# Loading x for a convolution by FFT: one chunk of the inverse per piece, and the last nine rows in one transfer per batch

## The chip, the cores and the metric

The kernel runs on one core of a Trainium2 chip. The metric is the time of one execution on that core in microseconds (us); lower is better. The core has a matrix engine (PE, with its weight loads shown apart as PEld), a vector engine (DVE), a scalar engine (ACT), a general engine (POOL) and a queue engine (SP), which run side by side and wait for each other through semaphores, and 16 DMA engines that move data for all of them.

## The reference

Two parts, one after the other. The first convolves each of 128 channels of `x` along the sequence with `h`, causally, by FFTs of twice the length. The second takes that result as its `x`, turns it by an angle, mixes it over the sequence with two matrices of 5696 x 5696 and ends with a small layer over the channels.

```python
batch, seq, d_model = (8, 5696, 128)
...
L = 2 * S
Xf = np.fft.rfft(x, n=L, axis=1)
Hf = np.fft.rfft(h, n=L, axis=0)
y = np.fft.irfft(Xf * Hf[None, :, :], n=L, axis=1)[:, :S, :]
...
theta = x @ w_theta
zr, zi = x * np.cos(theta), x * np.sin(theta)
y = np.einsum('ts,bsd->btd', w_tok_r, zr) + np.einsum('ts,bsd->btd', w_tok_i, zi)
u = x + y
return (u + np.maximum(u @ w_ch, 0.0)).astype(np.float32)
```

## The kernel before

The convolution takes the first 350 to 400 us of the span, and the change touches only this part. The sequence of 5696 is seen as 89 rows of 64, and the transform of length 11392 as 178 times 64. The work is cut into eight groups: a pair of batches and one half (64) of the channels. Each group goes through four stages.

- Stage a (`stage_a`, line 250): for each of the 64 channels one matmul takes the group's slice of x, 89 partitions by 128 columns (two batches of 64), against a table of 89 x 180. All four pieces of both batches must have landed before the first of these matmuls can run. ACT moves the results to the tile `a` (line 259).
- Stage b (`stage_b`, with `f2`, line 270): the second transform, in 12 chunks of up to 8 frequencies, each with 32 small matmuls. ACT moves a chunk to `xs` (line 426), and DVE multiplies it with the spectrum of h, `hs` (lines 428 and 433), into `uv`. `hs` comes from the scratch `hf_hbm` in HBM, 256 KB per chunk, by transfers of the SP queue (line 419). There are four buffers for `hs` (`LEAD`), so four chunks are loaded ahead and every further one starts when DVE has used an earlier one.
- Stage c (`stage_c`, lines 448 and 449): the first half of the inverse, in 16 chunks of 8 columns. Each chunk is moved to the tile `g` by DVE (line 455) or ACT (line 453).
- Stage d (`stage_d`, line 484): the second half of the inverse, in 7 chunks, moved to `yt` (lines 488 and 490) and stored to `yt_hbm` by eight transfers of the SP queue (line 497).

The loop over the groups has two halves. In the first half, stage c of group g is woven with stage a of group g+1, with the first four `hs` loads of group g+1 and with the loading of x for group g+2. In the second half, stage b of group g+1 is woven with stage d of group g. Below, "a stage c" and "a stage b" mean these halves, numbered by the loop. The helper `woven` sorts the steps of its lists by place: a list with (0.1, 1.02) is spread evenly from 10% to 102% of the half.

x is loaded by `load_x`. A group's tile `x16` has 89 partitions, two batches, 64 columns and 64 channels, in half precision, and there are two such tiles. The transfers convert from single precision, and POOL issues them. They come in eight pieces: four for each batch, 16 of the 64 columns each. A piece is two transfers, of the first 80 rows and of the last 9, and every row and column of it is a run of 64 numbers of its own. Before a piece of a group from the third on, POOL copies one number of `g` into the piece (line 151). This copy has no use but to wait: the transfer of the 80 rows, which writes over that number, can't start before the chunk of stage c that made it. The number is that of column `16 * i`, which is in chunk 2i, so piece i waits for chunk 2i. The 9 rows lie in other partitions, so they don't wait for it.

The queue of POOL runs in order. For the first two groups and in the first half of the loop's first turn, the order on DVE, ACT and POOL is that of the text. After that a planner puts each engine's instructions in order. It lets the 9-row transfers of a group run ahead of that group's copies, so that most of them stand at the end of the loop's first half one turn earlier. There they wait until stage a has read the tile that they overwrite (line 250). Every transfer that POOL issues also waits for the one eight before it, since eight semaphores are used in turn.

After the eight groups, the mixing over the sequence fills the rest of the span; its weights come in by POOL's transfers as well (line 676).

Of the kernel before, what the change touches and what calls it, by code (L numbers as in the profile page):

```python
# [22 lines left out]
def kernel(  # L23
# [10 lines left out]
    nc = tc.nc  # L34
    B, S, D = x.shape
# [40 lines left out]
    N2 = 64  # L76
    N1 = NF // N2
    NB = S // N2
    K1 = N1 // 2 + 1
    CK = 8  # L80
    HD = D // 2
# [48 lines left out]
    for p0, p1 in ((0, 80), (80, NB)):  # L130
        nc.gpsimd.dma_start(u_t[p0:p1, :N2 * D],
                            bass.AP(tensor=h.tensor, offset=h.offset + p0 * N2 * D,
                                    ap=[[N2 * D, p1 - p0], [1, N2 * D]]))
# [3 lines left out]
    def load_x(g, after=None):  # L137

        bp, dh = divmod(g, 2)
        if g >= B:  # L140
            return []
        if g not in x16s:
            x16s[g] = fx.tile([P, 2, N2, XP], F16, tag="x16", name="x16")
        x16 = x16s[g]

        def piece(i):
            e, n0 = i // 4, i % 4 * 16
            src = x[2 * bp + e]
            if after is not None:
                g_ = after["g"]  # L150
                nc.gpsimd.tensor_copy(x16[0:1, e, n0, 0:1], g_[0:1, 0, 16 * i:16 * i + 1])  # L151
            for p0, p1 in ((0, 80), (80, NB)):
                nc.gpsimd.dma_start(  # L153
                    x16[p0:p1, e, n0:n0 + 16, :HD],
                    bass.AP(tensor=src.tensor, offset=src.offset + (p0 * N2 + n0) * D + dh * HD,
                            ap=[[N2 * D, p1 - p0], [D, 16], [1, HD]]))
        return [lambda i=i: piece(i) for i in range(8)]

    ordered = ExitStack()
# [120 lines left out]
    def woven(*lists):  # L280

        lists = [l if isinstance(l, tuple) else (l, 0.0, 1.0) for l in lists]
        steps = [(w0 + (i + 0.5) / len(l) * (w1 - w0), n, f)
                 for n, (l, w0, w1) in enumerate(lists) for i, f in enumerate(l)]
        for _, _, f in sorted(steps, key=lambda s: s[:2]):
            f()
# [97 lines left out]
    def e_table(n):  # L384
        n0 = 11 * n
        t, k, r = ((e_y[0], e_f[1], e_y[0]), (e_y[1], e_y[0], e_y[1]), (e_f[2], e_y[1], e_y[0]))[n]
        nc.vector.tensor_scalar(k, t, MAGIC, None, op0=add)
        nc.vector.scalar_tensor_tensor(r, k, MAGIC, t, op0=ALU.subtract, op1=ALU.subtract)
        absolute(k, r)

        def curves():
            t3, k3 = (z.rearrange("p (n m) -> p n m", m=NB) for z in (r, k))
            sine(e_t[:K1, n0:n0 + 11, 1, :], t3, -1)
            cosine(e_t[:K1, n0:n0 + 11, 0, :], k3)
        return curves

    def swap_rows():
        for c0 in range(0, NCK, NCK // 2):
            for ri in range(2):
                dst, src = (hf_hbm[c0:c0 + NCK // 2, :, r0:r0 + 64, r, :].rearrange("c h p n -> (c h) p n")  # L400
                            for r0, r in ((64, ri), (0, 1 - ri)))
                nc.sync.dma_start(dst, src)
# [36 lines left out]
    def stage_c(st, last):  # L439

        def chunk(q):
            if q == 0:
                st["g"] = fg.tile([P, 2 * N2, P], F16, tag="g", name="g_")
            ps = psum()
            for i in range(8):
                o = ps[:, i // 4, (i % 4) * P:(i % 4 + 1) * P]
                at = (q + i) * K1
                nc.tensor.matmul(o, u_t[:, at:at + P], r_u, start=True, stop=False)  # L448
                nc.tensor.matmul(o[:, 2 * NP:], v_t[:, at:at + P], r_v, start=False, stop=True)  # L449
            g_out = st["g"][:K1, :, q:q + 8]  # L450
            g_in = ps[:K1].rearrange("p a (q c) -> p c (a q)", q=4)
            if (last and q % 16 == 0) or (not last and q % 32 == 16):
                nc.scalar.activation(g_out, g_in, AF.Copy)
            else:
                nc.vector.tensor_copy(g_out, g_in)
        return [lambda q=q: chunk(q) for q in range(0, 2 * HD, 8)]
# [48 lines left out]
    def front(g, by_dve=(), a_=None, spare=None):  # L505
        if g >= len(groups):
            return [], [], []
        bp, dh = groups[g]
        x16 = x16s[g].rearrange("p b n d -> p (b n) d")
        steps, a_st = stage_a(lambda q: x16[:NB, :, q], by_dve, a_, spare)  # L510
        return (steps, *stage_b(a_st, dh, WARM if g else WARM // 2, g == 0))
# [142 lines left out]
    def open_ring():  # L654

        ring["all"] = keep.tile([P, K1 * 3 * N2], BF16, tag="keep", name="ring")
        pump()
# [27 lines left out]
    def open_phases():  # L685
        st = sides["phases"] = {}
        sb1 = pool("s2", 2, pha, reuse_waits="tile")
        st["sb1"] = sb1
        st["zz"] = pool("s2z", ZB, pha, reuse_waits="tile")
        sbc = pool("s2c", 1, pha, reuse_waits="tile")  # L690
        for w_, dst, mul in ((moe_w_theta, w_theta_sb, 1.0 / (2.0 * math.pi)), (moe_w_ch, w_ch_sb, 1.0)):
            t = sbc.tile([P, P], F32, tag="wt", name="wt")
            nc.gpsimd.dma_start(t, w_[:, :])
            nc.gpsimd.tensor_scalar(dst, t, mul, None, op0=mult)
        ones = sbc.tile([P, P], BF16)
        nc.vector.memset(ones, 1.0)
        pm = sbc.tile([P, 2], BF16)
        nc.vector.memset(pm[:, 0:1], MAGIC / P)
        nc.vector.memset(pm[:, 1:2], -MAGIC / P)
        plus, minus = (pm[:, q:q + 1].to_broadcast([P, 512]) for q in range(2))  # L700
        w_neg = sbc.tile([P, P], BF16)
        nc.gpsimd.tensor_scalar(w_neg, w_theta_sb, -1.0, None, op0=mult)
        st["turns"] = (ones, plus, minus, w_neg)

    def load_ya0():
        sides["phases"]["ya0"] = only = ExitStack()
        ya = sides["phases"][0] = pool("s2a", 1, only, reuse_waits="tile").tile([P, 4, H], BF16, name="ya0")
        for p_ in range(4):
            nc.gpsimd.dma_start(ya[:, :, p_ * QR:p_ * QR + QR], yt_hbm[:, 0:4, p_ * QR:p_ * QR + QR])
# [54 lines left out]
    def with_load(step, load):  # L764
        def both():
            step()
            if load:
                ring["upto"] += 1
                pump()
        return both  # L770

    for g, (bp, dh) in enumerate(groups):
        st = {}
        last = g + 1 == len(groups)
        a_, load_, b_ = fronts.pop(g + 1) if g + 1 in fronts else front(g + 1)
        if last:
            for _ in range(3):
                steps0.pop(0)()
        now = ([with_load(steps0.pop(0), n < 6) for n in range(9)] if last else [], 0.0, 0.88)
        c_ = stage_c(st, last)  # L780
        if g == 0:
            ec = []
            swap_rows()
            now = ([lambda: ec.append(e_table(1)), lambda: ec.pop()(), lambda: ec.append(e_table(2)), lambda: ec.pop()(),
                    e_minus],
                   -0.1, 0.6)
        woven((c_, 0.06 if a_ else 0.0, 1.0), (a_, 0.0, 0.88), now, load_, (load_x(g + 2, st), 0.1, 1.02))
        if g == 0:
            ordered.close()
        if g + 2 == len(groups):  # L790
            xin.close()
            open_phases()
            load_ya0()
        now = [steps0.pop(0) for _ in range(5)] if last else []
        woven(b_, (stage_d(st, bp, dh, load_ya1 if last else None), 0.08 if b_ else 0.0, 1.1 if b_ else 1.0), now)
        if g + 2 == len(groups):
            load_ya1(st["yt"], True)
            open_ring()
# [305 lines left out]
    nxt, second, st = None, None, {}  # L1104
    ordered = ExitStack()
    for i, (k, p, tt, j0, s0, nj) in enumerate(stretches):
# [13 lines left out]
        if (p, tt, j0 + s0) == (0, 1, 0):  # L1120
            with tc.issue_after(sides["late"].ins):
# [4 lines left out]
        woven = (tt is not None and end_of_pair and i + 1 < len(stretches)  # L1126
                 and stretches[i + 1][2] is not None)
        held = a if i else None
        a, nxt = nxt, None if i == 1 else prepare(i + 1, not woven)
# [208 lines left out]
```

## Time and profile before

| | |
|---|---|
| median of 3 runs | 2052.54 us (2051.28 to 2053.35) |
| the profiled execution | 2052.18 us |
| its span in the profile | 2050.4 us |
| PE busy | 1959.6 us, 96% of the span |
| DVE, POOL, ACT busy | 1538.9, 965.2, 639.9 us |
| mean granted clock of PE | 0.987 |
| x's transfers (line 153) | 128, 97.9 us of POOL |
| of 80 rows | 64, 160 KB each, median 5.0 us from issue to landing |
| of 9 rows | 64, 18 KB each, median 4.7 us |
| the copies that wait (line 151) | 48, six groups of 8 |

Times are in us from the start of the span, unless marked ns. A line of the timeline has the start, the length, the engine, the line, the operation with what it writes and reads, how many were merged, and in square brackets how long the engine stood idle before and what ended that. "issue" there means that nothing the profile shows was waited for. A view by stretches of time gives the busy time of each engine in each stretch, the mean clock that was granted to PE, and the busy share of the 16 DMA engines, which goes above 1 where packets overlap on an engine. In a view of the DMA queues, q0 is POOL's transfers, q1 is those of SP, and q8 is the fetching of instructions.

### The profile page before, as it was taken

How to read it: one execution, taken by the hardware profiler on the slowest of the kernel's cores; microseconds unless marked ns; L12 is line 12 of the kernel's file. 1: busy time of each engine (PE TensorE's matmuls, PEld its weight loads, DVE VectorE, ACT ScalarE, POOL GpSimd, SP SyncE). 2: the span in 40 equal slices, each digit the busy share in tenths (PEclk: the TensorE clock that was granted, in tenths of full speed). 3: DMA queues.
4: the chain of work that ended last, by engine and by line, in shares of the span. 5: the costliest groups of instructions: out<-in, count | busy, mean ns of one | idle time of the engine just before them, and what ended most of it. 6: DMA issues, size and time to landing. Idle time of an engine off the chain costs nothing.

```text
span 2050.4 us, 42565 instructions
## 1 busy us (share of the span) xinstructions
PE 1959.6 (96%) x16205; PEld 1086.2 (53%) x16381; DVE 1538.9 (75%) x2806; ACT 639.9 (31%) x936; POOL 965.2 (47%) x1769
## 2 busy tenths in 40 slices
PE   7799899799999999999999998999999999999998
PEld 5688888654444444444444443444444444444444
DVE  7787777657788888787867667867777686777767
ACT  6788777872232333333300000011111111111111
POOL 8323312384354545454566454453544535354450
PEclk9899999999999999999999999999999999999999
DMA  9999996999899998999999799797887969788793
GB/s 151 187 180 159 146 171 204 238 293 179 163 179 176 170 180 159 179 173 177 170 168 159 119 251 217 107 152 131 150 145 132 155 124 153 131 150 146 131 156 85
DMA packets 510158, 338.21 MB, mean 165 GB/s; under 512 B 184136, under 2 KB 461256, under 8 KB 509864
## 3 DMA queue, kind: packets, MB, share of 16 engines
q0 software_dynamic: 322368, 157.47, 61.0%
q1 hardware_dynamic: 181600, 166.48, 27.8%
q10 hardware_dynamic: 5984, 11.54, 1.6%
q8 instruction: 128, 2.10, 0.4%
q14 instruction: 78, 0.63, 0.1%
HBM read 379.54 MB, written 95.63 MB: 232 GB/s over the span
## 4 chain that ended last, share of the span: by engine, by line
PE 66%; DVE 3%; DMA 2%; issue 1%; POOL 0%; ACT 0%; DVEq 0%; ACTq 0%; SPq 0%
PE m L1275 62%; DMA b<-z_hbm 1%; DVE c L1282 1%; DVE b L831 1%; PE v L977 1%; PE utp L970 1%; PE m L1279 1%; DVE wt L890 1%; PE theta_ps L560 0%; PE tpz L918 0%; PE m L1162 0%; PE m L1196 0%; POOL ring L676 0%; DMA c<-cp_hbm 0%; DMA wl<-in_moe_w_tok_i_dram 0%
## 5 line engine op out<-in xcount | busy, mean ns | idle before, releaser
L676 POOL DMA_DIRECT2D ring<-in_moe_w_tok_i_dram x720 | 387.9, 546 | 657.7 <-DVE wt L890 576.9
L890 DVE STREAM_TRANSPOSE wt<-ring 128x384 f32<-128x384 f32 (+2 forms) x720 | 360.5, 527 | 127.7 <-PE m L1275 77.7
L676 POOL DMA_DIRECT2D ring<-in_moe_w_tok_r_dram x720 | 386.2, 547 | 142.4 <-DVE wt L890 82.4
L1275 PE MATMUL m<-b,wt 128*128 128x512 bf16 x1605 | 386.6, 380 | 3.7 <-DVE wt L890 1.7
L1275 PEld LDWEIGHTS <-wt 128*128 128x128 bf16 x1804 | 176.3, 98 | 219.5 <-DVE wt L890 7.4
L1282 DVE TENSOR_TENSOR c<-c,m 128x512 f32<-128x512 f32 x412 | 266.8, 674 | 0.4 <-PE m L1275 0.4
L972 ACT ACTIVATE ring<-utp 128x512 bf16<-128x512 bf16 x85 | 50.8, 597 | 582.1 <-PE utp L970 582.1
L428 DVE TENSOR_TENSOR uv_t<-xs,hs 128x2048 f16<-128x2048 f16 x88 | 104.4, 1224 | 29.9 <-ACT xs L426 18.2
L448 PE MATMUL ps<-r_u,uv_t 128*128 128x128 f16 x1024 | 116.5, 219 | 4.7 <-ACT cos L588 1.3
L1196 PE MATMUL m<-b,wt 128*128 128x512 bf16 x471 | 110.3, 379 | 7.6 <-DMA b<-z_hbm 4.2
L967 ACT ACTIVATE ub<-c 128x512 bf16<-128x512 f32 x88 | 55.1, 628 | 192.1 <-DVE c L1237 113.5
L449 PE MATMUL ps<-r_v,uv_t 128*128 128x100 f16 x1024 | 114.1, 207 | 0.5
L153 POOL DMA_DIRECT2D x<-in_x_dram x128 | 97.9, 771 | 22.2 <-POOL x L151 14.9
L426 ACT ACTIVATE xs<-ps 128x1024 f16<-128x1024 f32 x96 | 90.8, 972 | 42.4 <-PE ps L270 21.9
L449 PEld LDWEIGHTS <-uv_t 128*128 128x128 f16 x1024 | 99.9, 98 | 7.1 <-issue 5.7
L448 PEld LDWEIGHTS <-uv_t 128*128 128x128 f16 x1024 | 100.0, 98 | 1.1 <-DVE uv_t L433 0.4
L1196 PEld LDWEIGHTS <-wt 128*128 128x128 bf16 x528 | 50.4, 98 | 65.1 <-issue 8.4
L562 ACT ACTIVATE red<-theta_ps,magic 128x512 f32<-128x512 f32 (+1 forms) x46 | 31.6, 687 | 153.1 <-PE theta_ps L560 80.4
L270 PEld LDWEIGHTS <-w_t 64*128 64x128 f16 x3240 | 59.4, 100 | 32.1 <-issue 23.3
L920 ACT ACTIVATE ring<-tpz 128x512 bf16<-128x512 bf16 (+1 forms) x46 | 27.5, 597 | 132.6 <-PE tpz L918 116.3
L250 PE MATMUL ps<-f_t,x 89*128 89x180 f16 x512 | 62.8, 252 | 2.1 <-DVE a L257 1.1
L831 DVE TENSOR_TENSOR b<-b 128x1024 bf16<-128x1024 bf16 x100 | 61.4, 685 | 0.0
(2924 smaller groups left out, 3746.7 us busy)
## 6 DMA issues: line engine op xcount, KB each, us to landing
ring<-in_moe_w_tok_r_dram POOLq DMA_DIRECT2D x352, 96.0 KB, 4.6
ring<-in_moe_w_tok_i_dram POOLq DMA_DIRECT2D x352, 96.0 KB, 4.9
ring<-in_moe_w_tok_r_dram POOLq DMA_DIRECT2D x352, 80.0 KB, 4.5
ring<-in_moe_w_tok_i_dram POOLq DMA_DIRECT2D x352, 80.0 KB, 4.0
cp_hbm<-c SPq DMA_DIRECT2D x88, 256.0 KB, 2.6
c<-cp_hbm SPq DMA_DIRECT2D x88, 256.0 KB, 4.5
out_dram<-c SPq DMA_DIRECT2D x88, 256.0 KB, 4.5
hs<-hf_hbm SPq DMA_DIRECT2D x84, 256.0 KB, 3.4
```

Source lines behind the costliest of these rows:

```text
L153: nc.gpsimd.dma_start(x16[p0:p1, e, n0:n0 + 16, :HD], bass.AP(tensor=src.tensor, offset=src.offset + (p0 * N2 + n0) * D + dh * HD, ap=[[N2 ...
L250: nc.tensor.matmul(ps[:, i // 2, (i % 2) * 2 * K1:(i % 2 + 1) * 2 * K1], lhs(q + i), f1_t[:NB], start=True, stop=True)
L426: nc.scalar.activation(xs[:, :, :, :ck], ps, AF.Copy)
L428: nc.vector.tensor_tensor(uv[:, :, :, c0:c0 + ck], xs.rearrange("p e d k -> p e (d k)").unsqueeze(1).to_broadcast([P, 2, 2, HD * CK]), hv. ...
L448: nc.tensor.matmul(o, u_t[:, at:at + P], r_u, start=True, stop=False)
L449: nc.tensor.matmul(o[:, 2 * NP:], v_t[:, at:at + P], r_v, start=False, stop=True)
L676: nc.gpsimd.dma_start(wb[32 * i:32 * i + 32, :ng, :nj * 64], bass.AP(tensor=a.tensor, offset=a.offset + row0 * S + p * H + i * QR + j0 * 6 ...
L831: return [lambda f=f, x=x: f(*x) for f, x in ((nc.vector.tensor_sub, (bt[M3], b12, b22)), (nc.vector.tensor_sub, (bt[M4], b21, b11)), (nc. ...
L890: nc.vector.transpose(wt.rearrange("p j t r -> p (j t r)").bitcast(F32).rearrange("p (j g t) -> p g j t", j=TJ, g=4)[:, :ng, :nj], wb[:, : ...
L1196: nc.tensor.matmul(ms[n // 2 * 2 + h], a[n][:, j, :, r], bts_of[p][jj][n % 2 * 2 + h][:, r, :], start=(n % 2 == 0 and jj == 0 and r == 0), ...
L1275: nc.tensor.matmul(ms[q], a[q][:, j, :, r], bts[jj][q][:, r, :], start=(jj == 0 and r == 0), stop=(jj == NJ - 1 and r == 1 and q not in left))
L1282: nc.vector.tensor_tensor(c, z, ms[q], op=op)
```

## The change

The number that a piece waits for is that of column `8 * i` in place of `16 * i`, so piece i waits for chunk i. The list of pieces is spread over 10% to 60% of the half in place of 10% to 102%. The first three pieces of a batch load 80 rows only, and with the fourth the last 9 rows of all 64 columns come in one transfer. A group has 10 transfers in place of 16, of the same bytes and the same runs.

```diff
             if after is not None:
                 g_ = after["g"]
-                nc.gpsimd.tensor_copy(x16[0:1, e, n0, 0:1], g_[0:1, 0, 16 * i:16 * i + 1])
-            for p0, p1 in ((0, 80), (80, NB)):
+                nc.gpsimd.tensor_copy(x16[0:1, e, n0, 0:1], g_[0:1, 0, 8 * i:8 * i + 1])
+            for p0, p1, a, w in ((0, 80, n0, 16), (80, NB, 0, N2))[:2 if i % 4 == 3 else 1]:
                 nc.gpsimd.dma_start(
-                    x16[p0:p1, e, n0:n0 + 16, :HD],
-                    bass.AP(tensor=src.tensor, offset=src.offset + (p0 * N2 + n0) * D + dh * HD,
-                            ap=[[N2 * D, p1 - p0], [D, 16], [1, HD]]))
+                    x16[p0:p1, e, a:a + w, :HD],
+                    bass.AP(tensor=src.tensor, offset=src.offset + (p0 * N2 + a) * D + dh * HD,
+                            ap=[[N2 * D, p1 - p0], [D, w], [1, HD]]))
         return [lambda i=i: piece(i) for i in range(8)]
...
-        woven((c_, 0.06 if a_ else 0.0, 1.0), (a_, 0.0, 0.88), now, load_, (load_x(g + 2, st), 0.1, 1.02))
+        woven((c_, 0.06 if a_ else 0.0, 1.0), (a_, 0.0, 0.88), now, load_, (load_x(g + 2, st), 0.1, 0.6))
```

In the two built programs the order of instructions on PE, DVE, ACT and SP is the same; only POOL's differs. In the turns from the second on, POOL has: the first four copies each followed by its 80-row transfer, then two copies, two transfers, two copies, two transfers, and at the end both 9-row transfers of the group that is loaded in the next turn, the first of which waits for stage a. In the first turn, where the order is by hand, the planner still puts the next group's 9-row transfers in: the first of them, which waits for stage a, stands behind the sixth copy and ahead of the sixth, seventh and eighth piece, as one of the smaller ones does before. The last two 9-row transfers of that kind fall away in the sixth turn in both programs, since there is no further group.

## The prediction

> **What bounds the kernel now.** First the view by stretches of time, cut where one loop half ends and the next begins (first and last matmul of line 449). PE is the engine to watch. The stages c from the second turn on last 17.46 us each, and PE is busy in all of it. The stages b that follow (rows below) differ:
>
> ```profile
> core 0: us, PE busy (x) PEld busy (x) DVE busy (x) ACT busy (x) POOL busy (x), PEclk, DMA share, GB/s
> 112.17:129.63 17.46, 17.46 (x310) 17.44 (x311) 12.96 (x11) 14.53 (x20) 8.09 (x16) 1.00 1.31 178
> 129.63:149.89 20.26, 17.95 (x571) 15.61 (x568) 16.80 (x16) 16.11 (x19) 5.21 (x9) 1.00 0.92 169
> ...
> 167.35:188.11 20.76, 17.99 (x571) 15.67 (x567) 16.81 (x16) 15.78 (x19) 4.96 (x9) 1.00 0.89 161
> ...
> 205.57:229.78 24.21, 20.23 (x571) 17.86 (x567) 16.97 (x16) 15.79 (x19) 4.95 (x9) 0.86 0.76 133
> ...
> 247.24:268.29 21.05, 17.70 (x571) 15.52 (x567) 16.87 (x16) 15.80 (x19) 4.95 (x9) 1.00 0.83 153
> ...
> 285.75:304.74 18.99, 17.78 (x570) 15.64 (x567) 16.78 (x16) 15.74 (x19) 1.66 (x3) 1.00 0.81 168
> ```
>
> The same 571 matmuls take 20.26, 20.76, 24.21, 21.05 and 18.99 us. The last, and shortest, is the one stage b into which POOL issues no row of nine (x3 in place of x9). Over it the four others hold 1.27 + 1.77 + 5.22 + 2.06 = 10.32 us.
>
> What the four wait for shows in the timeline of the weight loads, here in the longest:
>
> ```profile
> 210.11 0.89 PEld L484 LDWEIGHTS <-g__4597 90*128 90x128 f16 x21 [0.35 <-issue]
> 211.06 0.52 PEld L270 LDWEIGHTS <-w_t 64*128 64x128 f16 x32
> 211.64 1.25 PEld L484 LDWEIGHTS <-g__4597 90*128 90x128 f16 x30
> 212.96 0.72 PEld L270 LDWEIGHTS <-w_t 64*128 64x128 f16 x45
> 217.12 0.55 PEld L270 LDWEIGHTS <-w_t 64*128 64x128 f16 x19 [3.44 <-issue]
> ```
>
> PE stops in the middle of a run of equal loads, for "issue": it waits for no other engine. From 210.11 to the stop it took 21 + 32 + 30 + 45 = 128 loads, so with their matmuls 256 instructions. A 16 KB packet of q8 starts at 214.70 and takes 1.07 us, and PE goes on 1.35 us after its end. I counted all loads and semaphore steps of PE up to each stop: the stops at 140.1, 144.6, 175.0, 178.9, 213.7, 255.6, 328.0 and 335.6 stand at place 193 or 194 of 256, and each ends 1.35 to 1.71 us after a 16 KB packet of q8. So PE runs out of instructions. In stage b it uses 256 in 3.4 to 4 us; in stage c (311 loads in 17.46 us) in 7.2 us, and there it never stops.
>
> The view of the DMA queues for 206.3 to 213.8 says what the fetch stands behind:
>
> ```profile
> q0 software_dynamic: 4141, 0.43, 97.4%
> q1 hardware_dynamic: 333, 0.62, 33.6%
> q8 instruction: 1, 0.02, 0.8%
> ...
> x<-in_x_dram POOLq DMA_DIRECT2D x6, 18.0 KB, 5.7
> ```
>
> x's small runs fill the engines, and `hs` lands behind them. q0's last packets come 9.2, 8.9, 10.3 and 8.6 us after the end of stage c in those four turns, and 5.3 us in the sixth, where no fetch is late.
>
> **The change, part by part.** POOL's timeline of the second turn gives the prices:
>
> ```profile
> 118.97 0.18 POOL L151 COPY x<-g__2471 1x1 f16<-1x1 f16 x1 [1.00 <-DVE g__2471 L455]
> 119.49 0.89 POOL L153 DMA_DIRECT2D x<-in_x_dram  x1 [0.34 <-POOL x L151]
> ...
> 127.73 0.61 POOL L153 DMA_DIRECT2D x<-in_x_dram  x1 [0.70 <-PE ps L250]
> ...
> 130.41 4.43 POOL L153 DMA_DIRECT2D x<-in_x_dram  x7
> ```
>
> *The wait for chunk i.* A piece costs POOL 0.18 + 0.34 + 0.89 = 1.41 us, and chunks come every 17.46 / 16 = 1.09 us, so POOL sets the pace. The first copy stays at 114.47 and the eighth piece is issued by 114.47 + 8 x 1.41 = 125.8, where it is now issued at 131. Two pieces wait for a copy of the next one (1 us); the limit of eight transfers in flight is not reached before the tail.
>
> *Nine rows in one transfer.* POOL issues 10 per group in place of 16. One of 576 runs is not in the trace: between 0.61 us (144 runs) and 0.89 (1280) I take 0.72, by the line between. The two of the next group wait for stage a at 127.73 as one does now, and are out at 129.2; seven more transfers now take until 134.8. Behind them in POOL's queue stands only the next turn's copy, 15 us later. In all POOL saves 48 x 0.61 - 16 x 0.11 = 27.5 us, which lies beside PE's work and is worth nothing by itself.
>
> *When x is in.* Up to 122 SP's stores and `hs` loads share the engines: q0 has 2216 packets from 117 to 122. Of a group's 12544, 10328 are left, at 946 per us (2838 from 122 to 125) or 731 (2193 from 126 to 129): done at 132.9 to 136.1, so 3.3 to 6.5 us after stage c, about where the sixth turn has it. The `hs` loads of stage b start at 134, and the late fetches were 7.6 to 10.5 us after stage c. So I set the four stages b near 18.99. Least: only stops that begin while q0 still has packets go, 0.93 + 3.44 + 2.80 = 7.2. Most: all 10.3. I take -8.7, the middle.
>
> *The first turn.* There the 9-row transfer that waits for stage a blocks three pieces until 88.0, now and then. What follows is the same bytes, issued by 88.0 + 3 x (0.89 + 0.72) + 2 x 0.18 = 93.2 in place of 97.7. This stage b (22.26 us) waits mostly in the order between PE and ACT; its one stop at place 194 is 0.49. I take -0.4, between -3.3 (down to 18.99) and +1.0 (a stop like that at 140.1).
>
> *The start.* The first group's 16 transfers take POOL 13.09 us, and ten will take 13.09 - 6 x 0.61 = 9.4; the second group is issued from 23.3 on and not from 26.96. The engines are idle there (65 packets of q0 from 23.9 to 28.2). Four us at the 566 per us of 28.2 to 42 move 2300 packets forward, out of the 4737 that now share 42 to 54.7 with the stores and loads of h's spectrum. DVE starts there on
>
> ```profile
> 54.69 4.74 DVE L428 TENSOR_TENSOR uv_t<-xs,hs 128x2048 f16<-128x2048 f16 x4 [4.53 <-DMA hs<-hf_hbm]
> ```
>
> This wait and the next (1.44) can give up to 6.0 us. Against that, PE has two stops in fetching at 24.0 and 27.3 (1.50 and 2.13) while q0 is idle, and x now flows there: up to +3.6. I take -2.5.
>
> The rest of the span runs after this in the same order; I take 0. Sum: -8.7 - 0.4 - 2.5 = -11.6. The profiled execution took 2052.18 us (2050.4 and 1.8 around it), 0.36 under the median, so the forecast is 2040.6.
>
> [...]
>
> **The rivals.**
>
> 1. *x is not out in time.* With eight transfers in flight and `hs` among them, x drains until 8 us after stage c, as now. For: 946 per us was held for 3 us only, and 4491 packets from 130 to 138.9 are 505 per us. Against: there POOL issued seven transfers of 144 runs at 0.63 us each, 230 per us, so the issue set that pace. Half the first term and 1 us of the start are left: 2052.18 - 4.4 - 1.0 = 2046.8.
>
> 2. *The stops are not x's doing.* For: the stops at 144.6 and 178.9 come 5.8 and 2.6 us after q0's last packet, and that at 328 has no x near. Against: the sixth turn has none. The start alone remains: 2052.18 - 2.5 = 2049.7.
>
> 3. *Slower: the fetch is late in stage c too.* With pieces every 1.41 us q0 is never empty there. [...] For: the DMA share in stage c goes from at most 1.54 toward what two pieces at once make (2.16 from 122 to 125). Against: at 2.16 no stop is seen in any stage c, and there the next packet of q8 comes in time.
>
> That the change does not do what it says is excluded: its orders are in the built program.
>
> **How the numbers follow.** The forecast 0.60, rivals 0.16, 0.12 and 0.12. 0.2% (4.1 us) is what a measurement here can tell from no change, so faster means under 2048.4. Faster: 0.58 of the forecast, 0.11 of the first rival, 0.03 of the second: 0.72. Slower, over 2056.3: 0.10 of the third and 0.01 of the second: 0.11. The same: 0.17. The range goes from the most of all terms, 2052.18 - 10.3 - 3.3 - 6.0 = 2032.6, taken as 2033, to 2050.5, just above the second rival. It leaves out the third and the edges.
>
> **What would show it.** The stages b of turns two to five at 19.0 to 19.8 us, with no stop at place 194 over 0.6 us; q0 empty within 6.5 us of the end of stage c; stages c still 17.46; POOL's eighth piece at 11 to 13 us after the first copy; DVE's first line 428 before 52.5. It is wrong if the stops stay with q0 empty (rival 2), if q0 goes on to 8 us (1), or if stage c grows (3). [...]

## The result, and the profile after

| | before | after |
|---|---|---|
| median, us | 2051.36 (22 runs) | 2057.82 (22 runs) |
| ratio after / before | | 1.0033, 95% interval 1.0020 to 1.0047 |
| profiled execution, span, us | 2050.4 | 2054.4 |
| first stage c starts, us | 70.75 | 69.22 |
| stages b of turns two to six, sum, us | 105.3 | 108.9 |

The change made the kernel slower by 0.33%. 2040.6 us was forecast, with a range from 2033 to 2050.5, and the time lies above both. The program moved as the diff says: the order of the instructions on PE, DVE, ACT and SP is the same as before, and only POOL's queue differs.

The view by stretches of time of the changed kernel, with a stage c first and then the stages b of turns two to six:

```profile
core 0: us, PE busy (x) PEld busy (x) DVE busy (x) ACT busy (x) POOL busy (x), PEclk, DMA share, GB/s
111.54:129.01 17.47, 17.47 (x310) 17.45 (x311) 12.97 (x11) 14.51 (x20) 10.06 (x18) 1.00 2.15 191
129.01:152.02 23.01, 19.37 (x571) 16.99 (x568) 16.89 (x16) 16.16 (x19) 0.00 (x0) 0.93 1.07 139
169.49:192.12 22.63, 20.71 (x571) 18.36 (x568) 16.88 (x16) 16.19 (x19) 0.00 (x0) 0.85 0.92 129
209.59:230.40 20.81, 18.09 (x571) 15.60 (x568) 16.79 (x16) 15.65 (x19) 0.00 (x0) 1.00 0.86 141
247.87:269.09 21.22, 17.87 (x570) 15.60 (x568) 16.93 (x16) 15.87 (x19) 0.00 (x0) 1.00 1.07 140
286.55:307.82 21.27, 18.07 (x570) 15.57 (x568) 16.88 (x16) 15.65 (x19) 0.00 (x0) 1.00 0.62 136
```

Stage c is as long as before (17.47 us, before 17.46), with PE busy in all of it, although the DMA share in it rose from 1.31 to 2.15: the crowding there costs nothing there. POOL now issues nothing in the stages b (x0). Yet none of them comes down to 18.99. The fourth turn's is 3.4 us shorter than before, the fifth's is as it was (21.22 for 21.05), and the other three are 1.9 to 2.8 us longer.

POOL's timeline of the second turn shows the early pieces, as forecast:

```profile
113.83 0.18 POOL L151 COPY x<-g__2453 1x1 f16<-1x1 f16 x1 [21.50 <-DVE g__2453 L455]
114.35 0.91 POOL L153 DMA_DIRECT2D x<-in_x_dram  x1 [0.34 <-POOL x L151]
...
122.51 1.78 POOL L153 DMA_DIRECT2D x<-in_x_dram  x2 [0.18 <-POOL x L151]
127.12 1.62 POOL L153 DMA_DIRECT2D x<-in_x_dram  x2 [2.83 <-PE ps L250]
```

The eighth piece is issued by 124.3, 10.5 us after the first copy, and the two transfers of nine rows by 64 for the next group go out back to back from 127.12 (0.81 us each, where 0.72 was forecast). q0's last packets come 5.4, 5.8, 5.1, 6.6 and 2.4 us after stage c in turns two to six, where they came after 9.2, 8.9, 10.3, 8.6 and 5.3. So x did leave the queue sooner. The weight loads of the third turn still stop:

```profile
171.07 1.10 PEld L484 LDWEIGHTS <-g__3510 90*128 90x128 f16 x26 [0.46 <-issue]
172.25 0.87 PEld L270 LDWEIGHTS <-w_t 64*128 64x128 f16 x56
174.72 0.18 PEld L270 LDWEIGHTS <-w_t 64*128 64x128 f16 x8 [1.60 <-issue]
```

This stop is again at place 194 of 256. The instruction packet before it starts at 170.83 and takes 2.34 us; in these stages of the kernel before such packets took 0.89 to 1.66. The view of the DMA queues from 169.5 to 174, in which the two merged transfers drain (40 slices; the DMA row is the busy share in tenths):

```profile
DMA  9999999999999999999999999999999999799999
GB/s 67 92 101 107 100 125 129 117 104 90 79 207 58 45 17 14 33 21 19 11 11 21 18 18 13 16 21 23 21 14 21 27 34 31 16 29 117 153 244 244
...
q0 software_dynamic: 2293, 0.20, 226.4%
q1 hardware_dynamic: 39, 0.08, 7.7%
q8 instruction: 1, 0.02, 3.3%
```

From the 15th slice to the 36th the share stays at 0.7 or more, and 11 to 34 GB/s move: until 173 about 140 runs (packets of 128 bytes) per us, each taking about 210 ns in the mean, where a run took 32 ns in the tail before. The instruction packet and `hs` (q1) are under way at the same time. The fifth turn has such a packet too (2.35 us from 250.69, before a stop of 1.59); in the fourth the longest took 1.88, and in the second and the sixth at most 1.16. Below, "the stops" are the waits of 0.3 us or more at places 193 and 194 in the stages b of turns two to six. They sum to 14.9 us, against 11.1 before.

At the start, DVE's first line 428 moved as forecast, from 54.69:

```profile
52.47 4.74 DVE L428 TENSOR_TENSOR uv_t<-xs,hs 128x2048 f16<-128x2048 f16 x4
```

and PE's weight loads stopped in fetching instead:

```profile
39.85 0.23 PEld L270 LDWEIGHTS <-w_t 64*128 64x128 f16 x7 [4.00 <-issue]
```

This stop is at place 194 of 256 as well: a 16 KB packet of q8 starts at 37.40 and takes 0.90 us, and PE goes on 1.55 us after its end. The wait of 4.53 us for `hs` is gone; one stop of 4.00 us on PE took most of its place, and the first stage c starts 1.53 us earlier.

### The profile page after: what moved, and what is told of

It is laid out like the page before. It is cut to its first block, busy times and chain, and to the rows that moved or that the text cites. A ratio compares the mean times of both kernels' runs of the same rounds, so it can differ in the third digit from the quotient of the medians.

```text
span 2054.4 us, 42516 instructions
## 1 busy us (share of the span) xinstructions
PE 1960.5 (95%) x16205; PEld 1086.9 (53%) x16381; DVE 1536.3 (75%) x2806; ACT 639.6 (31%) x936; POOL 939.7 (46%) x1721
## 4 chain that ended last, share of the span: by engine, by line
PE 68%; DVE 3%; issue 1%; DMA 1%; POOL 1%; ACT 0%; DVEq 0%
PE m L1275 62%; PE m L1196 2%; DVE c L1282 1%; PE v L977 1%; PE utp L970 1%; PE m L1279 1%; DVE b L831 1%; DVE wt L890 1%; POOL ring L676 0%; PE theta_ps L560 0%; PE tpz L918 0%; PE m L1162 0%; DMA ring<-in_moe_w_tok_i_dram 0%; DMA y_hbm<-ring 0%; DMA wl<-in_moe_w_tok_i_dram 0%
## 5 line engine op out<-in xcount | busy, mean ns | idle before, releaser
L449 PEld LDWEIGHTS <-uv_t 128*128 128x128 f16 x1024 | 100.3, 98 | 6.5 <-issue 4.9
L153 POOL DMA_DIRECT2D x<-in_x_dram x80 | 73.6, 923 | 28.2 <-PE ps L250 15.6
```

The source lines that it names most:

```text
L153: nc.gpsimd.dma_start(x16[p0:p1, e, a:a + w, :HD], bass.AP(tensor=src.tensor, offset=src.offset + (p0 * N2 + a) * D + dh * HD, ap=[[N2 * D ...
```

## The experiments

The expectations speak of three theories. A: the early 80-row pieces crowd the queue in and after stage c. B: the merged 9-row transfers hold up the instruction fetches and the `hs` loads. C: the stops in stage b are not x's doing. A block is a run of 256 of PE's instructions: the profile of the kernel before has 128 packets in q8 and 16381 weight loads, each with its matmul, so 256 to a packet. "Ratio" is the time over that of the kernel before on the same chip. One profile of the same turns scatters by several us (the last experiments show it), so verdicts rest on the ratios. In all twelve runs the order of the instructions on PE, DVE, ACT and SP is that of the kernel before; only POOL's differs.

### One half of the change at a time

*The merge alone*, with waits and places as before (here and below the start and length of a transfer follow `a` and `w`, as in the change):

```diff
-            for p0, p1 in ((0, 80), (80, NB)):
+            for p0, p1, a, w in ((0, 80, n0, 16), (80, NB, 0, N2))[:2 if i % 4 == 3 else 1]:
```

> Only the 9-row transfers are merged; the waits and the places in the loop's first half stay those of the kernel before. Theory A (crowding: pieces that come every 1.4 us pile up in the queue of x at the end of stage c, and the instruction fetches of the last block of c and the first of stage b come late): ratio to before 0.998 to 1.001, share of the DMA engines in stage c about 1.4 as before. Theory B (the merged transfers: 1152 runs into nine partitions drain slowly, 85 to 150 runs per us in the trace of after, and hold up fetch and hs): ratio 1.003 or more, with a slow tail of q0 in every turn that has two 9x64 transfers at its end. Theory C (the stops do not hang on x at all): ratio 1.000.

Measured: 1.0035 (1.0023 to 1.0048), so 7.2 us (4.7 to 9.8). The whole loss is here, and the stops sum to 15.6 us. But the slow tail that theory B expected is not: in the last 3 us of q0 the median run takes 32 ns in every turn. Here is the first of the four longest stops (2.55, 2.55, 2.10 and 1.91 us):

```profile
142.14 0.84 PEld L270 LDWEIGHTS <-w_t 64*128 64x128 f16 x53 [2.55 <-issue]
```

The instruction packets before these four take 1.12 to 1.27 us, no longer than in the kernel before. They start late, 7.5 to 8.4 us after stage c and 0.02 to 0.64 us before PE runs out, where the long packet of the changed kernel's third turn started 2.3 us before. The longest stop of the kernel before, of 3.44 us, is of this kind too: its packet starts 1.02 us after PE ran out.

*The earlier wait and place alone*, with the 9 rows in four transfers:

```diff
-                nc.gpsimd.tensor_copy(x16[0:1, e, n0, 0:1], g_[0:1, 0, 16 * i:16 * i + 1])
+                nc.gpsimd.tensor_copy(x16[0:1, e, n0, 0:1], g_[0:1, 0, 8 * i:8 * i + 1])
...
-        woven((c_, 0.06 if a_ else 0.0, 1.0), (a_, 0.0, 0.88), now, load_, (load_x(g + 2, st), 0.1, 1.02))
+        woven((c_, 0.06 if a_ else 0.0, 1.0), (a_, 0.0, 0.88), now, load_, (load_x(g + 2, st), 0.1, 0.6))
```

> Only the earlier pieces (chunk i, places 10% to 60%); the 9 rows come in four transfers per batch as before. Theory A: ratio 1.003 or more, share of the DMA engines in stage c about 2.2, fetch packets of the last block of stage c 2.5 us or more after the block's start. Theory B: ratio 0.995 to 0.998, no slow tail, since 32 ns per run stays possible at the end. Theory C: 1.000.

Measured: 0.9996 (0.9985 to 1.0007). Theory A falls as a cause of the loss, and so does the gain that I had put on the earlier wait. q0 ends 4.2, 6.8, 7.3 and 6.8 us after stage c in turns two to five, 2 to 5 us sooner than before, for nothing: the stops sum to 11.4 us (11.1 before).

### What x costs at all, and the merged rows at another place

*No x from the third group on*: the tile of the group two before is used again, so the output is not the reference's.

```diff
+        if g >= 2:
+            x16s[g] = x16s[g - 2]
+            return []
```

> x from the third group on is not loaded; the tiles of the first two groups are read again, so the output is not the reference's. Theories A and B: the stages b of turns one to six fall to about 19 us with hardly a stop at place 193 or 194, and the time to 2052 - 13 = 2039 (ratio 0.993 to 0.995). Theory C: the stops stay (0.5 to 1.5 us, one or two per stage b, beside hs alone), stages b of 20 to 22 us, ratio 0.998 to 1.001.

Measured: 0.9969 (0.9959 to 0.9980). All of x's loads from the third group on cost 0.31% of 2050 us, 6.4 us (4.1 to 8.4). That is less than theories A and B expected and more than C did. The stages b are 19.08, 19.24, 18.78, 18.89 and 18.97 us, with stops of 0.3 to 1.0 us that sum to 4.5. So theory C holds for the small stops, which stay with no x under way, and not for the long ones.

*The merged rows with the first piece of a batch*, in stage c, in place of the last (their wait is a second copy, of one number in each of partitions 64 to 88):

```diff
+            if after is not None and i % 4 == 0:
+                nc.gpsimd.tensor_copy(x16[64:NB, e, n0, 0:1], g_[64:NB, 0, 8 * i:8 * i + 1])
-            for p0, p1, a, w in ((0, 80, n0, 16), (80, NB, 0, N2))[:2 if i % 4 == 3 else 1]:
+            for p0, p1, a, w in ((0, 80, n0, 16), (80, NB, 0, N2))[:2 if i % 4 == 0 else 1]:
```

> After's kernel, but the merged 9-row transfer of a batch goes with its first piece instead of its fourth and waits for the same chunk, by a second copy of 25 numbers, so that no 9-row transfer of the next group stands at the end of stage c. Theory A: still crowded, ratio to before 1.002 or more. Theory B: the slow drain falls into stage c, where a fetch has 7.2 us, so ratio 0.995 to 0.998. Theory C: 1.000.

Measured: 1.0055 (1.0040 to 1.0069). That is no remedy, and theory B missed here. The stops sum to 12.9 us. Moving the transfer also changed POOL's order (in the second turn five pieces went behind copies of later ones), so this run doesn't price the place alone, and it doesn't show why it is slower than the change.

### The 9 rows by themselves

*Only the 9-row transfers from the third group on, merged* (no 80-row pieces, no copies; the output is not the reference's):

```diff
+            rows = slice(0, 2) if after is None else slice(1, 2)
-            for p0, p1, a, w in ((0, 80, n0, 16), (80, NB, 0, N2))[:2 if i % 4 == 3 else 1]:
+            for p0, p1, a, w in ((0, 80, n0, 16), (80, NB, 0, N2))[:2 if i % 4 == 3 else 1][rows]:
```

> From the third group on the 80-row pieces of x and their copies are left out; only the 9-row transfers of 64 values of n2, one per batch, are loaded (the output is not the reference's). Theory B (the merged 9-row transfers themselves hold up the fetches and hs, whatever else of x is under way): they cost as much alone as beside the pieces, so about 0.35% above the kernel with nothing of x loaded (0.9969): 1.0000, between 0.999 and 1.002, and clearly above the run with the 9 rows in four. Theory A2 (they cost only as the tail behind the pieces, in a full queue): about 0.997 to 0.998, level with that run.

*The same in four* (the output is not the reference's):

```diff
+            rows = slice(0, 2) if after is None else slice(1, 2)
-            for p0, p1 in ((0, 80), (80, NB)):
+            for p0, p1 in ((0, 80), (80, NB))[rows]:
```

> As the run before, but the 9 rows go in four transfers of 16 values of n2 per batch, at the places they have in the kernel before (the output is not the reference's). Theory B: 0.997 to 0.998, 0.002 or more below the run with the merged rows. Theory A2: 0.997 to 0.998 as well, within 0.001 of it. If the 9 rows are what x costs in any form, 0.9985 to 1.000.

Measured: merged 1.0002 (0.9992 to 1.0012), in four 0.9969 (0.9958 to 0.9981). In four, the rows cost nothing that can be told from no x at all; merged, the same bytes cost 0.33%, with none of the pieces near. Theory A2 falls. The DMA queues in the third turn, merged (167.6 to 172) and then in four (168.4 to 172.4):

```profile
DMA  9999999999999487966676659323141002559549
GB/s 91 98 134 102 55 55 54 64 83 228 83 54 23 6 7 6 7 5 5 5 6 6 6 5 7 2 2 4 2 5 1 0 0 93 186 186 279 149 168 354
...
q0 software_dynamic: 1363, 0.12, 79.2%
...
q8 instruction: 1, 0.02, 4.7%
```

```profile
DMA  9534547933988234157555369946987233644835
GB/s 72 31 19 6 25 29 49 222 16 9 50 53 50 15 12 9 9 38 46 37 28 20 12 31 73 58 22 25 53 51 44 15 5 13 41 29 26 54 23 164
...
q0 software_dynamic: 1736, 0.13, 57.3%
q8 instruction: 1, 0.02, 2.2%
```

Merged, the queue's 1363 packets take 79.2% of the engines' time; in four, 1736 take 57.3%. From 169 to 171 a run takes 240 ns in the mean when merged, and 32 ns in four. The one instruction packet in the first of these takes 3.29 us and in the second 1.39. In turns two to five the first one after stage c takes 1.66, 3.29, 2.50 and 1.85 us merged, and at most 1.39 in four. What that does to PE in the merged run, third turn (line 268 there is line 270 elsewhere):

```profile
169.96 0.93 PEld L268 LDWEIGHTS <-w_t 64*128 64x128 f16 x59
173.14 0.14 PEld L268 LDWEIGHTS <-w_t 64*128 64x128 f16 x5 [2.26 <-issue]
```

The five stages b sum to 105.1 us merged and 96.4 in four. Of the 8.7 us, 2.5 are stops (8.0 against 5.5), and 5.5 are two stages in which the granted clock fell to 0.86 and 0.85 and PE was busy 20.67 and 20.49 us in place of 17.8.

*Half the merge*: two transfers of 32 per batch, waits and places as before.

```diff
+            for p0, p1, a, w in ((0, 80, n0, 16), (80, NB, n0 - 16, 32))[:2 if i % 2 else 1]:
```

> The kernel before with the 9 rows of a batch in two transfers of 32 values of n2, in place of four of 16 or one of 64; waits and places as before. Theory B, with the price rising with the length of one transfer: between 1.0000 and 1.0035, about 1.001 to 1.002. If the price has a threshold between 16 and 64: either 0.9995 to 1.0005 or 1.003 to 1.004. If the loss is the place of the transfers in the queue (last of a batch) and not their length: about 1.0035 x a half, not told apart from the first.

Measured: 1.0021 (1.0007 to 1.0036), between four transfers and one, as a price that rises with the length of a transfer would have it. The interval is too wide to exclude a threshold, and the place of the transfers in the queue is not told apart from their length.

### POOL's order by hand

Before and after, the planner puts several 9-row transfers of the next group one behind the other at the end of stage c. Here POOL's order is the written one from turn two to six, so that the 9 rows (in four) follow each their own 80-row transfer; the waits are those of the change:

```diff
-        if g == 0:
+        if g in (0, 5):
             ordered.close()
+        if g == 0:
+            ordered.enter_context(tc.manual_schedule(engines={mybir.EngineType.Pool}))
```

> Pieces wait for one chunk each and sit early, as in the change; the 9 rows stay in four transfers, each right behind its own 80-row transfer, in an order of POOL's written by hand for turns one to five, so that rows don't gather behind the end of stage c. If what drains after stage c makes the late fetches: x is out 2 us after stage c or earlier, each stage b is 19 to 20 us, ratio 0.995 to 0.998. If the stops need only hs: 0.9985 to 1.0005. If x beside the transfers of stage c is a cost of its own (weights and fetches there), above 1.001.

Measured: 0.9978 (0.9966 to 0.9989), a real gain. The stops sum to 6.1 us, and q0 ends 3.6 to 5.6 us after stage c, later than the 2 us of the expectation. The next two share the frame of this one. *By hand, with the late waits of the kernel before* (`16 * i`, 1.02):

> POOL's order by hand as in the run that beat the kernel before (0.9978), but each piece waits for two chunks, as in the kernel before. If the earlier wait for one chunk is what empties the queue sooner: x ends 8 us or more after stage c as before, ratio 0.999 to 1.001. If the gain came from the hand-written order alone (no row of nine issued behind the end of stage c for the next group): 0.9975 to 0.9985.

Measured: 0.9970 (0.9956 to 0.9983). So the order makes the gain and the earlier wait adds nothing. POOL's timeline shows why: a piece with its rows costs 2.0 us of POOL's time and more, so POOL sets the pace and a copy waits 0.45 us for its chunk, now and then:

```profile
116.86 1.51 POOL L153 DMA_DIRECT2D x<-in_x_dram  x2 [0.30 <-POOL x L151]
...
123.02 0.18 POOL L151 COPY x<-g__2473 1x1 f16<-1x1 f16 x1 [0.45 <-DVE g__2473 L455]
```

The stages b of turns two to six, in the columns of the first table of stretches:

```profile
129.10:149.08 19.98, 17.85 (x570) 15.64 (x567) 16.88 (x16) 15.87 (x19) 2.20 (x4) 1.00 0.85 167
166.56:185.32 18.76, 17.79 (x571) 15.70 (x567) 16.80 (x16) 15.76 (x19) 2.62 (x5) 1.00 0.82 167
202.80:223.48 20.68, 17.91 (x570) 15.53 (x567) 16.89 (x16) 15.76 (x19) 2.41 (x5) 1.00 0.85 156
240.96:262.10 21.14, 19.07 (x570) 16.91 (x567) 16.97 (x16) 15.64 (x19) 2.19 (x4) 0.92 0.78 152
279.58:298.48 18.90, 17.69 (x570) 15.63 (x568) 16.79 (x16) 15.77 (x19) 2.81 (x5) 1.00 0.84 168
```

They sum to 99.5 us (105.3 before, and 100.3 in a second profile of the same turns, below), and q0 ends 4.6 to 5.5 us after stage c, although the copies wait as long as before. *By hand, with the change's waits and its merged rows*:

> The change with POOL's order by hand: the merged 9-row transfer of a batch follows the fourth 80-row piece of that batch, none runs ahead at the end of stage c. Theory B (the merged transfer costs wherever it lies): 1.001 to 1.004, well above the 0.9978 of the same order with the 9 rows in four. If the changed kernel lost only because the planner put two merged transfers back to back behind stage c: 0.997 to 0.999.

Measured: 0.9997 (0.9986 to 1.0008), against 0.9978 with the rows in four. The two differ by 0.19% in the same order, with intervals that overlap from 0.9986 to 0.9989. So the merge seems to take the gain away even with no two merged transfers back to back; the stops sum to 12.7 us.

### The start and the turns apart

*The merge in the loads of the first two groups alone*:

```diff
+            for p0, p1, a, w in (((0, 80, n0, 16), (80, NB, n0, 16)) if after is not None else
+                                 ((0, 80, n0, 16), (80, NB, 0, N2))[:2 if i % 4 == 3 else 1]):
```

> Only the loads of the first two groups, before any turn, have their 9 rows merged (one transfer of 64 per batch); from turn one on waits, places and transfers are those of the kernel before. The prediction's start term alone is -2.5 us: ratio 0.9988. Theory B (a merged transfer holds up fetches and hs loads behind it): the first two groups meet no stage b and few hs loads, so the start may gain 0 to 2.5 us (0.9988 to 1.0000), or lose 1 to 2 us if its PE stops in fetching (24 to 40 us) grow as they did in the changed kernel (one of 4.00): up to 1.001.

*The change in the turns alone* (`after is None` in that line, with the change's waits and place):

> The change in the turns alone; the first two groups are loaded as in the kernel before. If the loss sits in the turns (theory B): 1.003 to 1.005, the changed kernel's 1.0033 plus what its start gains. If the start lost and the turns gained as forecast: 0.995 to 0.997.

Measured: start alone 0.9995 (0.9982 to 1.0008), turns alone 1.0046 (1.0030 to 1.0063). The loss sits in the turns. The start is worth -1.0 us, between -3.7 and +1.6, which tells it neither from nothing nor from the -2.5 forecast. The first of the two has the turns of the kernel before; its stages b sum to 100.3 us and its stops to 7.5, where the other profile of these turns had 105.3 and 11.1. So much do single profiles scatter.

### All of them side by side

| order of POOL | wait | 9 rows | ratio (95%) | stops in five stages b, us |
|---|---|---|---|---|
| planner | two chunks | 4 x 16 | 1 | 11.1, 7.5 |
| planner | one chunk | 4 x 16 | 0.9996 (0.9985 to 1.0007) | 11.4 |
| planner | two chunks | 2 x 32 | 1.0021 (1.0007 to 1.0036) | 12.0 |
| planner | two chunks | 1 x 64 | 1.0035 (1.0023 to 1.0048) | 15.6 |
| planner | one chunk | 1 x 64 (the change) | 1.0033 (1.0020 to 1.0047) | 14.9 |
| planner | one chunk | 1 x 64, in the turns alone | 1.0046 (1.0030 to 1.0063) | 12.4 |
| planner | one chunk | 1 x 64, with the first piece | 1.0055 (1.0040 to 1.0069) | 12.9 |
| by hand | one chunk | 1 x 64 | 0.9997 (0.9986 to 1.0008) | 12.7 |
| by hand | one chunk | 4 x 16 | 0.9978 (0.9966 to 0.9989) | 6.1 |
| by hand | two chunks | 4 x 16 | 0.9970 (0.9956 to 0.9983) | 6.5 |
| planner | none; no 80-row pieces | 1 x 64 | 1.0002 (0.9992 to 1.0012) | 8.0 |
| planner | none; no 80-row pieces | 4 x 16 | 0.9969 (0.9958 to 0.9981) | 5.5 |
| | no x | | 0.9969 (0.9959 to 0.9980) | 4.5 |

Merging costs 0.2 to 0.4% in each pair that differs in it alone, the earlier wait does nothing in each pair, and the written order gains 0.2 to 0.4% in each. The version by hand with two chunks and 4 x 16 beats both kernels, and is level with no x at all.

## Why the prediction was wrong

- **The view of the bound was right.** PE stops in stage b for instructions that come late, and x is a cause: without it 0.31% goes, and the long stops with it.
- **The step that failed** is the cost of "*Nine rows in one transfer*". I counted POOL's issues alone ("*lies beside PE's work and is worth nothing by itself*") and took its bytes into the drain as if they were any others. Merged, they are not: this term, put at nothing, measured +7.2 us (1.0035, 4.7 to 9.8 us), and the rows by themselves agree (1.0002 against 0.9969). That the merge makes the loss is shown, and that PE loses the time in its stops and with a lowered clock. How it makes the instructions late is shown in part. In the changed kernel and with the rows by themselves the runs took 210 and 240 ns in the stretches above, and instruction packets among them up to 2.35 and 3.29 us; in the run with the merge alone the runs took 32 ns, and the packets came late in their start.
- **"*So I set the four stages b near 18.99*"** fell with it, and was mis-sized too. Draining was forecast at 3.3 to 6.5 us after stage c and came at 5.1 to 6.6 in turns two to five; the stops stayed. I read "x out at 5.3 us, no stop" off one stage b, the sixth turn's, and that one differs in two things: x is out sooner, and POOL issues no row of nine for a next group behind stage c. I chose the first. The run with the earlier wait alone moved the first by 2 to 5 us for nothing (-0.8 us, between -3.1 and +1.4), and those with the written order, which removes the second, gained 0.22% and 0.30%. Why the gathered transfers cost that is not shown. The term of -8.7 us was also more than all of x costs (6.4 us, 8.4 at most).
- **The first turn.** -0.4 was forecast, within -3.3 and +1.0; its stage b grew from 22.26 to 23.28 in the one profile, just past the upper bound.
- **The start.** -2.5 was forecast. All the steps came (the second group's x issued from 23.2, DVE's first line 428 at 52.47, the `hs` wait gone), and PE's larger stop, which I had as a risk of up to 3.6 us, gave most of it back: -1.53 us in the profile, -1.0 (-3.7 to +1.6) in the runs.
- **The rivals.** "*x is not out in time*" is wrong, since it was. "*The stops are not x's doing*" is right for the small ones alone. "*Slower: the fetch is late in stage c too*" had the sign and not the place: no stage c has a stop at a DMA share of 2.15. No rival held the merged transfer to be at fault. No row showed a 9 x 64 transfer; I bounded what POOL pays to issue one, and never what it does to a packet that comes behind it.
- **The clock** had no term in the forecast, and it is a part of the cost: see below.

What stays open: why a run of a merged transfer can take over 200 ns, why the packets start late where it doesn't, and whether four transfers of 16 at the very place of a merged one would cost the same. No run here shows which DMA engine a packet ran on, and none laid the nine rows out otherwise than in transfers of 16, 32 or 64 columns.

## What to carry to other kernels

Fewer and longer transfers saved the issuing engine's time here (0.81 us for the nine rows of a batch, in place of four times 0.61) and still cost the kernel 0.35%. Before merging small ones, look at what else is under way at that moment, instruction fetches above all, and price the drain from a row of the same shape. Here PE uses 256 instructions in 3.4 to 4 us in stage b, and late fetches stopped it for up to 3.44 us at a time in the kernel before; how early x left the queue did not decide it. And when one stage is the good example, list all that sets it apart before choosing one of them as the cause.

## What the runs showed that I had not expected

*A stop that lowers the clock.* In 14 profiles there are 70 stages b of turns two to six. In the 45 whose longest stop at place 193 or 194 is 1.59 us or less, the granted clock is 1.00 in every one and PE is busy 17.5 to 18.1 us. Of the 25 with a stop of 1.60 us or more, 20 have a clock of 0.80 to 0.93, and PE is busy 19.0 to 22.1 us. So such a stop costs its own length and then mostly 1.2 to 4 us more. The half-clock stretches (a granted clock of 0.50) in the two traces of before and after are 3.41 us long or two to four times that. In each of the 14 traces all of them start on one grid with a step of 3.413 us, and what seems to decide is how much of one step the stops take. In these turns 20 steps at full clock were followed by half clock, and PE stood in stops for 1.43 to 2.68 us of each; in the other 662 it stood for at most 1.66. The five long stops without a lowered clock lie across a grid line, as the one at 255.6 before: its 2.80 us fall into 1.55 and 1.25. Of the 20 lowered clocks 18 go with stops shorter than one step, from 1.60 us on, so here PE had to stand for only about half a step.

*Early draining by itself is worth nothing.* In turns two to five the queue of x ended 8.6 to 10.3 us after stage c or 4.2 to 7.3, with the same time (0.9996, 0.9985 to 1.0007), so long as the same transfers of nine rows were issued one behind the other at the end of stage c.
